# Spectra by pairs of k1, one step for k1 = 32, raw weights on another queue: a change to a fused S4D convolution and gated unit

## The chip, the cores and the metric

The kernel runs on one NeuronCore of a Trainium2 chip. TensorE (PE) multiplies matrices into PSUM, VectorE (DVE), ScalarE (ACT) and GpSimd (POOL) work elementwise, and SyncE (SP) issues DMAs. ACT and POOL issue DMAs as well, each from a queue of its own. Every engine takes its instructions in the program's order. The metric is device time in microseconds (us); the profile is one execution, as the hardware profiler recorded it.

## The reference

The input `u` has 2048 positions of 448 channels. It is normalized, and two branches are added to it.

```python
xn = _layernorm(x)
# S4D: a kernel of 2048 taps for each channel, from 256 complex modes
P = exp((A * dt[:, None])[:, :, None] * pos[None, None, :])
K = 2.0 * einsum("dn,dnl->dl", C, P).real
y = irfft(rfft(xn_t, 2 * L) * rfft(K, 2 * L))[..., :L]      # causal convolution
a = y + xn * D_skip
# gated unit: 448 -> 1792 -> 448
b = (sigmoid(xn @ w_gate) * (xn @ w_up)) @ w_down
out = x + a + b
```

All inputs and the output are float32.

## The kernel before

Two generators in Python emit the program. `conv()` emits the convolution, `glu()` the gated unit. The loop at the end of the kernel always advances the one whose done share of its total is smaller; each `yield` carries a weight (`WK`, `WS`, `WP`, `WX` and so on) that is added to what is done. So the weights and the two totals decide how the two branches lie beside each other on PE. A scheduler then orders the instructions of each engine from that emission; `issue_after` pins some of them behind a named instruction.

**The convolution.** The transform of 4096 points is split in 64 x 64. `x_pair` and `x_spec` make the first stage of the input's transform and store it as `x1_d`. `rest(q)` loads blocks 8 to 15 of the input early and takes their statistics with `x_stats`. `kgen` generates the taps in 56 chunks: POOL builds magnitudes (`me`, `mf`, line 467), ACT sines (`S`), DVE their products `Et` and `Ft` (lines 520 to 522), and PE multiplies these into `ko` (line 532). After every fourth chunk the taps get their skip term (line 545, `ks`) and go through the first stage of their transform (line 559) to `sk_d`.

`spectra` does the rest for each half `h` of the channels (224 each) and for the 33 values of k1. A step has four values of k1; k1 = 32 is a step by itself in each half, so there are 18 steps. In a step `loads` fetches the two first-stage spectra (`sx`, `skl`) and a table; `there` transforms both (line 808), copies the taps' part to SBUF (`kc`, line 815), multiplies on DVE (lines 823 to 825); `back` transforms the product back (line 838), copies it (`vt`, line 845) and stores it from ACT's queue to `v_d` (line 854). `back` of a step is emitted ahead of `there` of the next. `turned` loads `v_d` into another layout (line 860), and `last` does the final transform of a half (line 871) and adds it to the result.

The bank of PSUM that `there` fills holds one part (real or imaginary) of two values of k1 for each 64 partitions. Six operations follow, each on 448 columns: four products, a subtraction, an addition.

**The gated unit.** The positions are worked on in two halves of 1024 and the 1792 hidden columns in 14 tiles of 128, in groups of 3, 3, 3, 3 and 2. `gate` runs 22 matmuls for each tile and 512 positions (line 638; float32 is split in a high and a low part), then tanh, product and split on ACT and DVE. Line 738 projects down after each group. In the first half the split weights are stored (`wt_d`, `dt_d`) and in the second reloaded, except for the tiles in `RAW`: their raw weights are loaded again on SP's queue (lines 576 to 584) and split on POOL (lines 692 to 715). One buffer, `wraw`, serves raw gate, up and down weights of all these tiles in turn. `ORDER` gives the groups' order in each half. Near the end of the second half the gated unit yields `None` and is held until the convolution has emitted everything.

Of the kernel before, what the change touches and what calls it, by code (L numbers as in the profile page):

```python
# [30 lines left out]
WS = 4  # L31
HOLE = 6
WS = 4
# [12 lines left out]
RAW = set(GROUPS[0] + GROUPS[1])  # L46
ORDER = [GROUPS, GROUPS[2:] + GROUPS[:2]]
# [8 lines left out]
def _tables():  # L56
# [17 lines left out]
    for q in range(NK1):  # L74
# [52 lines left out]
def s4d_glu_kernel(ctx, tc, io):  # L127
# [442 lines left out]
    def w_load(f, raw=None):  # L570
# [3 lines left out]
        for i, nm in enumerate(("B_w_gate", "B_w_up")):  # L574
            w = io[nm]
            nc.sync.dma_start(raw[:, i, 0:3], w[0:384, fs].rearrange("(k p) f -> p k f", p=128))
            for h in range(2):
                nc.sync.dma_start(raw[64 * h : 64 * h + 64, i, 3], w[384:448, fs])
        return raw

    def rd_load(f, rd=None):
        if rd is None:
            rd = pg.tile([128, D], F32, name="rd", bufs=RB)
        nc.sync.dma_start(rd, io["B_w_down"][128 * f : 128 * f + 128])
# [72 lines left out]
    def glu():  # L657
        for half in range(2):
# [4 lines left out]
            for fs_ in ORDER[half]:  # L663
# [10 lines left out]
                for f, t in order:  # L674
                    if t == 0:
# [14 lines left out]
                        elif f in RAW:  # L690
                            raw, wl = w_load(f), w_low()
# [8 lines left out]
                    if t == 0:  # L700
# [62 lines left out]
    def spectra(pf):  # L763
# [9 lines left out]
        def loads(h, k):  # L773
            ds, gs = slice(H * h, H * h + H), slice(7 * h, 7 * h + 7)
            sx = pf.tile([128, 4, H], F32, name="sx", bufs=NLD)
            sk = pf.tile([128, 7, 4, 32], F32, name="skl", bufs=NLD)
            if k == 32:
                nc.sync.dma_start(sx[:64, 0], x1_d[32, :, ds])
                nc.sync.dma_start(sk[:, :, 0], sk_d[:, gs, 32])
                return t32, sk, sx  # L780
            nc.sync.dma_start(sx[0:64], x1_d[k : k + 4, :, ds].rearrange("k b d -> b k d"))
# [13 lines left out]
        def there(k, ks, tb, sk, sx):  # L795

            np_, nj = (128, 2) if len(ks) > 1 else (64, 1)
            sp = {}
            for src, tag in ((sk, "ko"), (sx, "tr")):
                for c in range(2):  # L800
                    ps = bank("sp")
                    with after():
                        for n, (k1, i, j) in enumerate(ks):
                            kk = 64 if k1 in (0, 32) else 128
                            to, rhs = ps[64 * i : 64 * i + 64, j], sx[:kk, n]
                            if tag == "ko":
                                to, rhs = to.rearrange("p (g d) -> p g d", d=32), sk[:kk, :, n]
                            mm = nc.tensor.matmul(  # L808
                                to, tb[:kk, n, 64 * c : 64 * c + 64], rhs, start=True, stop=True,
                                skip_group_check=True,  # L810
                            )
                    sp_mm[:] = [mm]
                    if tag == "ko":
                        kc = pf.tile([128, 2, H], F32, name="kc", bufs=3)
                        nc.scalar.copy(kc[:np_, :nj], ps[:np_, :nj])  # L815
                        ps = kc
                    sp[tag, c] = ps
            o = (slice(0, np_), slice(0, nj))
            ys_ = [pf.tile([128, 2, H], F32, name="yy", bufs=4) for _ in range(2)]
            pd = [pf.tile([128, 2, H], F32, name="pd", bufs=2) for _ in range(2)]  # L820
            for c, to in ((0, ys_), (1, pd)):
                for e in range(2):
                    v.tensor_tensor(to[(c + e) % 2][o], sp["ko", e][o], sp["tr", c][o], ALU.mult)  # L823
            v.tensor_tensor(ys_[0][o], ys_[0][o], pd[0][o], ALU.subtract)
            v.tensor_tensor(ys_[1][o], ys_[1][o], pd[1][o], ALU.add)
            return ys_

        def back(h, k, ks, ys_):
            vt = pf.tile([128, 2, 2, H], F32, name="vt", bufs=2)
            bt = t32[:, 1:3] if k == 32 else bk  # L830
            n = min(2, len(ks))
            pvs = [bank("pv") for _ in range(n)]
            for p in range(0, len(ks), 2):
                for e in range(2):
                    for k1, i, j in ks[p : p + 2]:
                        s = slice(64 * i, 64 * i + 64)
                        with after():
                            mm = nc.tensor.matmul(  # L838
                                pvs[i][:, j], bt[s, e], ys_[e][s, j], start=(e == 0), stop=(e == 1),
                                skip_group_check=True,  # L840
                            )
                    sp_mm[:] = [mm]
            for i in range(n):
                nj = 2 if n == 2 else 1
                nc.scalar.copy(vt[:, i, :nj], pvs[i][:, :nj])


            for k1, i, j in ks:
                r = 32 if k1 == 32 else 8 * (k1 % 4) + k1 // 4
                if k1 in (0, 32):  # L850
                    to, fr = v_d[h, r::64], vt[0:128:2, i, j]
                else:
                    to, fr = v_d[h, r::32], vt[:, i, j]
# [199 lines left out]
```

## Time and profile before

| quantity | value |
|---|---|
| median of 3 runs | 843.39 us (840.48 to 846.02) |
| the profiled execution | 842.75 us, span 841.0 us |
| PE busy | 746.3 us, 89% of the span |
| DVE busy | 570.4 us, 68% |
| ACT busy | 401.1 us, 48% |
| POOL busy | 385.9 us, 46% |
| granted PE clock, mean | 0.939 |
| DMA | 112.83 MB, 134 GB/s in the mean |

The span runs from the first to the last instruction; the profiled execution has 1.75 us around it. The start lasts until the chunks of `kgen` begin near 140 us, these run to 608 us, the steps of `spectra` from 616 to 817 us, and the end to 841 us. PE and PEld are matmuls and their weight loads; a float32 matmul leaves two records, so eight matmuls stand as x16. The granted clock is the share of full speed that PE was given.

### The profile page before, as it was taken

To read this page: it belongs to the slowest core of one execution; us is meant where nothing else is said; L and a number is where in the kernel's file an instruction comes from. 1 tells how busy PE (TensorE), PEld (TensorE's weight loads), DVE (VectorE), ACT (ScalarE), POOL (GpSimd) and SP (SyncE) were. 2 spreads that over 40 slices of the span, in tenths; PEclk is the share of its full clock that TensorE was granted. 3 is DMA by queue.
4 is the path that set the end of the run, shared out by engine and by line. 5 is a ranking of instruction groups with operands and counts; after the bars stand their busy time and mean duration, and the time that the engine had idled before them with its cause. 6 is when DMAs were issued, how large, how long until landed. Compare 5 with 4: busy or idle time off the path is not lost.

```text
span 841.0 us, 18294 instructions
## 1 busy us (share of the span) xinstructions
PE 746.3 (89%) x7416; PEld 575.0 (68%) x7416; DVE 570.4 (68%) x766; ACT 401.1 (48%) x615; POOL 385.9 (46%) x390
## 2 busy tenths in 40 slices
PE   1999969988998987999999999999979998899766
PEld 1767758767886865666788778887746776466544
DVE  5598887887688989587489777789513443443333
ACT  2647445646658476675565666646412222122110
POOL 1100256875986996646376867778210021100002
PEclk9998979989999998699999999999979999699888
DMA  9444563343144443357432221220398898567536
GB/s 215 116 122 122 143 193 120 117 148 107 39 144 140 129 129 100 78 167 201 156 109 67 103 85 56 70 69 27 98 262 216 216 222 201 134 165 184 145 90 167
DMA packets 94467, 112.83 MB, mean 134 GB/s; under 512 B 12320, under 2 KB 83104, under 8 KB 94000
## 3 DMA queue, kind: packets, MB, share of 16 engines
q1 hardware_dynamic: 80272, 91.46, 39.9%
q10 hardware_dynamic: 13328, 18.47, 6.8%
q0 software_dynamic: 784, 1.74, 0.7%
q8 instruction: 58, 0.95, 0.5%
q14 instruction: 25, 0.20, 0.1%
HBM read 69.07 MB, written 42.57 MB: 133 GB/s over the span
## 4 chain that ended last, share of the span: by engine, by line
PE 49%; DVE 15%; DMA 9%; issue 8%; ACT 7%; POOL 7%; ACTq 2%; SPq 1%; POOLq 0%; DVEq 0%
PE gu L638 19%; PE po L738 8%; PE tr L483 5%; PE ko L532 4%; PE sp L808 4%; PE pv L838 4%; POOL me L467 3%; PE kp L559 3%; DVE Et L521 2%; ACTq L854 2%; DVE Et L520 2%; DVE Ft L522 2%; DMA wraw<-in_B_w_up_dram 1%; DVE pm L408 1%; DMA acc_d<-acc 1%
## 5 line engine op out<-in xcount | busy, mean ns | idle before, releaser
L467 POOL TENSOR_TENSOR me<-me,pm 128x32 f32<-128x32 f32 (+3 forms) x168 | 170.0, 1014 | 95.9 <-DVE Et L521 81.0
L467 POOL TENSOR_TENSOR mf<-mf,pm 128x64 f32<-128x64 f32 (+3 forms) x112 | 127.8, 1143 | 5.6
L638 PE MATMUL gu<-xh,wh 128*128 128x512 f32 x336 | 103.5, 414 | 7.4 <-DVE hf L647 6.9
L520 DVE TENSOR_TENSOR Et<-me,S 128x1024 f32<-128x1024 f32 x56 | 88.5, 1580 | 31.4 <-ACT S L495 28.0
L638 PE MATMUL gu<-xh,wl 128*128 128x512 f32 x336 | 98.6, 400 | 0.0
L638 PE MATMUL gu<-xl,wh 128*128 128x512 f32 x336 | 96.4, 393 | 0.0
L522 DVE TENSOR_TENSOR Ft<-mf,S 128x1024 f32<-128x1024 f32 x56 | 86.0, 1536 | 9.9 <-PE ko L532 7.6
L823 DVE TENSOR_TENSOR yy<-kc,sp 128x448 f32<-128x448 f32 (+1 forms) x36 | 20.8, 590 | 106.0 <-ACT kc L815 88.5
L738 PE MATMUL po<-dh,hh 128*128 128x448 f32 x224 | 84.9, 379 | 3.7 <-DVE hf L647 1.9
L638 PEld LDWEIGHTS gu<-xh,wh 128*128 128x128 f32 x336 | 63.8, 197 | 29.3 <-DVE hf L647 7.4
L738 PE MATMUL po<-dl,hh 128*128 128x448 f32 x224 | 83.4, 373 | 0.0
L521 DVE TENSOR_TENSOR Et<-me,S 128x1024 f32<-128x1024 f32 x56 | 82.9, 1480 | 0.7 <-POOL mf L467 0.7
L738 PE MATMUL po<-dh,hl 128*128 128x448 f32 x224 | 82.8, 372 | 0.1
L492 ACT ACTIVATE S<-tr 128x1024 f32<-128x1024 f32 x56 | 57.5, 1027 | 50.3 <-PE tr L483 47.0
L483 PE MATMUL tr<-sel,ph 128*128 128x512 f32 x224 | 69.7, 433 | 9.0 <-ACT S L494 8.6
L638 PEld LDWEIGHTS gu<-xh,wl 128*128 128x128 f32 x336 | 65.1, 194 | 14.5
L638 PEld LDWEIGHTS gu<-xl,wh 128*128 128x128 f32 x336 | 63.7, 190 | 13.6
L532 PEld LDWEIGHTS ko<-Et,Ft 128*32 128x32 f32 x3584 | 56.2, 112 | 23.5 <-issue 15.8
L532 PE MATMUL ko<-Et,Ft 128*32 128x64 f32 x3584 | 68.2, 224 | 2.8 <-DVE Ft L522 2.8
L743 DVE SCALAR_TENSOR_TENSOR acc<-po,acc 128x448 f32<-128x448 f32 x80 | 48.2, 616 | 29.2 <-PE po L738 28.2
L495 ACT ACTIVATE S<-S,hpi 128x1024 f32<-128x1024 f32 x56 | 65.4, 1167 | 0.0
L652 ACT CAST hh<-hf 128x512 fp32r<-128x512 f32 x56 | 34.8, 622 | 63.0 <-DVE hf L647 61.0
(176 smaller groups left out, 1265.9 us busy)
## 6 DMA issues: line engine op xcount, KB each, us to landing
sk_d<-sk ACTq DMA_DIRECT2D x14, 528.0 KB
sx<-x_d SPq DMA_DIRECT2D x32, 224.0 KB
skl<-sk_d SPq DMA_DIRECT2D x16, 448.0 KB
vp<-v_d SPq DMA_DIRECT2D x16, 448.0 KB
v_d<-vt ACTq DMA_DIRECT2D x62, 112.0 KB
wt_d<-wh SPq DMA_DIRECT2D x8, 512.0 KB
wt_d<-wl SPq DMA_DIRECT2D x8, 512.0 KB
wh<-wt_d SPq DMA_DIRECT2D x8, 512.0 KB
```

The costliest lines, as they stand in the source:

```text
L467: nc.gpsimd.tensor_tensor(m[:, :, w : 2 * w], m[:, :, 0:w], par(base + i).unsqueeze(2).to_broadcast([128, 4 * DC, w]), ALU.mult,)
L483: nc.tensor.matmul(ps[:, h], ph[:, cn % 2, 128 * h : 128 * h + 128], sel[:, i], start=(i == 0), stop=(i == 1),)
L492: nc.scalar.activation(rows(cs), pv, AF.Abs)
L495: nc.scalar.activation(cs, cs, AF.Sin, scale=-TWO_PI, bias=hpi)
L520: v.tensor_tensor(Et[:, :, :, 32:64], two(me[:, :, 32:64]), S[:, 1::-1], ALU.mult)
L521: v.tensor_tensor(Et[:, :, :, 0:32], two(me[:, :, 0:32]), S[:, 1:3, :, ::-1], ALU.mult)
L522: v.tensor_tensor(Ft, two(mf), S[:, 3:5], ALU.mult)
L532: nc.tensor.matmul(ko[32 * j : 32 * j + 32, sl], Ft[:, cc, DC * h + 4 * q + j], Et[:, cc, DC * h + 4 * q + j], start=(k == 0), stop=(k == ...
L638: glu_mm[:] = [nc.tensor.matmul(ps, a_, b_, start=(n == 0), stop=(n == len(mm) - 1))]
L652: nc.scalar.copy(hh, hf)
L738: glu_mm[:] = [nc.tensor.matmul(po, a_[:, bs], w_, start=(n == 0), stop=(n == 3 * fc - 1))]
L743: v.scalar_tensor_tensor(acc[:, b], po, 0.5, acc[:, b], ALU.mult, ALU.add)
```

## The change

Six edits are made together.

1. In a step of `spectra` the values of k1 go by pairs: a bank holds both parts of one pair. The taps' copy `kc`, the products and the sums are made for each pair. Two products of 448 columns give both parts' terms (one reads the bank with its parts swapped), and a subtraction and an addition of 224 columns combine them: eight operations a step in place of six.
2. k1 = 0 uses 128 rows like the others; its table has zeros in the lower 64.
3. k1 = 32 is one step for both halves of the channels, the second of 17 steps.
4. Raw weights of the second half are loaded from POOL's queue. `RAW` loses its fourth tile, and the second half does group 1 before group 0.
5. `rest` is a generator: its load is issued a turn earlier, and its statistics follow in the next turn, behind the last gate's product.
6. `WS` goes from 4 to 4.5, and the convolution's total counts 11 preparation turns and 17 steps in place of 9 and 18.

```diff
-WS = 4
+WS = 4.5
...
-RAW = set(GROUPS[0] + GROUPS[1])
-ORDER = [GROUPS, GROUPS[2:] + GROUPS[:2]]
+RAW = set(GROUPS[0] + GROUPS[1][1:])
+ORDER = [GROUPS, GROUPS[2:] + GROUPS[1::-1]]
...
+    tab[0, 64:] = 0.0
...
-                            raw, wl = w_load(f), w_low()
+                            raw, wl = w_load(f, eng=nc.gpsimd), w_low()
...
-                            rd = rd_load(f, pg.tile([128, D], F32, name="rdw", tag="wraw", bufs=1))
+                            rd = rd_load(f, pg.tile([128, D], F32, name="rdw", tag="wraw", bufs=1), nc.gpsimd)
...
             if k == 32:
-                nc.sync.dma_start(sx[:64, 0], x1_d[32, :, ds])
-                nc.sync.dma_start(sk[:, :, 0], sk_d[:, gs, 32])
+                nc.sync.dma_start(sx[:64, 0:2].rearrange("b h d -> b (h d)"), x1_d[32])
+                for i in range(2):
+                    nc.sync.dma_start(sk[:64, :, i], sk_d[:64, 7 * i : 7 * i + 7, 32])
                 return t32, sk, sx
...
+        def there(k, tb, sk, sx):
+            kk, np_ = (64, 64) if k == 32 else (128, 128)
+            ys_ = []
+            for j in range(2):
+                ks = [(0, j, 0)] if k == 32 else [(2 * j + i, 2 * j + i, i) for i in range(2)]
+                pss = []
+                for src in (sk, sx):
+                    ps = bank("sp")
+                    with after():
+                        for c in range(2):
+                            for t, n, i in ks:
+                                to, rhs = ps[64 * i : 64 * i + 64, c], sx[:kk, n]
+                                if src is sk:
+                                    to, rhs = to.rearrange("p (g d) -> p g d", d=32), sk[:kk, :, n]
+                                mm = nc.tensor.matmul(
+                                    to, tb[:kk, t, 64 * c : 64 * c + 64], rhs, start=True, stop=True,
+                                    skip_group_check=True,
+                                )
+                    sp_mm[:] = [mm]
+                    pss.append(ps)
+                    if src is sk:
+                        kc = pf.tile([128, 2, H], F32, name="kc", bufs=3)
+                        nc.scalar.copy(kc[:np_], ps[:np_])
+                yy = pf.tile([128, 2, H], F32, name="yy", bufs=4)
+                pd = pf.tile([128, 2, H], F32, name="pd", bufs=2)
+                xt = pss[1]
+                v.tensor_tensor(yy[:np_], kc[:np_], xt[:np_], ALU.mult)
+                v.tensor_tensor(pd[:np_], kc[:np_], xt[:np_, ::-1], ALU.mult)
+                v.tensor_tensor(yy[:np_, 0], yy[:np_, 0], yy[:np_, 1], ALU.subtract)
+                v.tensor_tensor(yy[:np_, 1], pd[:np_, 0], pd[:np_, 1], ALU.add)
+                ys_.append(yy)
+            return ys_
...
-        steps = [(h, k) for h in range(2) for k in (32, *range(0, 32, 4))]
+        steps = [(h, k) for h in range(2) for k in range(0, 32, 4)]
+        steps[0:2] = [steps[1], (None, 32), steps[0]]
...
                     x_load(xt, 4 * q, 4, [nc.sync])
-                    for b in range(4):
-                        x_stats(sm, 4 * q + b, xt[:, b])
+                    yield
+                    with tc.issue_after(hfs[-1].ins):
+                        for b in range(4):
+                            x_stats(sm, 4 * q + b, xt[:, b])
+                    yield
...
-                    if n in (5, 7):
-                        rest((n - 1) // 2)
+                    if n in (4, 6):
+                        more = rest(n // 2)
+                    if n >= 4:
+                        next(more, None)
...
-    total = [sum(Y0) + 9 * WP + 8 * WX + 4 + NCK * WK + HOLE + 18 * WS, 2 * (4 + NFT * 14.8) - HELD]
+    total = [sum(Y0) + 11 * WP + 8 * WX + 4 + NCK * WK + HOLE + 17 * WS, 2 * (4 + NFT * 14.8) - HELD]
```

More of the change, by code (lines that the diff above doesn't have):

```diff
@@ L30 @@
 WK = 5
-WS = 4
+WS = 4.5
 HOLE = 6
-WS = 4
+WS = 4.5
 WP = 5
@@ L568, in kgen, with w_load @@
                 yield WK
-    def w_load(f, raw=None):
+    def w_load(f, raw=None, eng=nc.sync):
         fs = slice(128 * f, 128 * f + 128)
@@ new lines, in there, with back @@
+                v.tensor_tensor(yy[:np_, 0], yy[:np_, 0], yy[:np_, 1], ALU.subtract)
+                v.tensor_tensor(yy[:np_, 1], pd[:np_, 0], pd[:np_, 1], ALU.add)
+                ys_.append(yy)
+            return ys_
+        def back(h, k, ys_):
+            vt = pf.tile([128, 2, 2, H], F32, name="vt", bufs=2)
+            bt, n = (t32[:, 1:3], 1) if k == 32 else (bk, 2)
+            pvs = [bank("pv") for _ in range(n)]
+            with after():
+                for j in range(2):
+                    for e in range(2):
+                        for i in range(n):
+                            s = slice(64 * i, 64 * i + 64)
@@ L817, in there @@
[L817 to L842, printed above, removed]
-            for i in range(n):
[L844 to L853, printed above, removed]
-                nc.scalar.dma_start(to.rearrange("r w d -> w r d"), fr)
@@ new lines, in back @@
+            sp_mm[:] = [mm]
+            for i in range(n):
+                nc.scalar.copy(vt[:, i], pvs[i])
+            for j in range(2):
+                for i in range(n):
+                    k1 = k + 2 * j + i
+                    if k == 32:
+                        to, fr = v_d[j, 32::64], vt[0:128:2, 0, j]
+                    elif k1 == 0:
+                        to, fr = v_d[h, 0::64], vt[0:128:2, i, j]
+                    else:
+                        to, fr = v_d[h, 8 * (k1 % 4) + k1 // 4 :: 32], vt[:, i, j]
+                    nc.scalar.dma_start(to.rearrange("r w d -> w r d"), fr)
@@ L894, in spectra @@
         for n, (h, k) in enumerate(steps):
-            ks = [(32, 0, 0)] if k == 32 else [(k + 2 * j + i, i, j) for j in range(2) for i in range(2)]
             sp_mm[:] = glu_mm
@@ L899, in spectra @@
                 back(*prev)
-            cur = there(k, ks, *ld[n])
+            cur = there(k, *ld[n])
             if n + NLD < len(steps):
```

31 lines of the change are left out of this document (8 added, 23 removed).

## The prediction

> **What bounds the kernel now.** I read the page first, then the busy time in stretches of 20 us, then the chain of work that ended last, and the timeline of single steps.
>
> ```profile
> span 841.0 us, 18294 instructions
> PE 746.3 (89%) x7416; PEld 575.0 (68%) x7416; DVE 570.4 (68%) x766; ACT 401.1 (48%) x615; POOL 385.9 (46%) x390
> PEclk9998979989999998699999999999979999699888
> ```
> ```profile
> 480.00:500.00 20.00, 20.00 (x264) 15.99 (x253) 15.78 (x14) 13.32 (x19) 16.84 (x15) 1.00 0.25 91
> 800.00:820.00 20.00, 12.51 (x78) 10.28 (x79) 7.19 (x13) 3.61 (x8) 0.00 (x0) 0.83 0.32 85
> ```
>
> PE is the bound, but not everywhere. In the kernel-generation stage (columns: window, busy PE, PEld, DVE, ACT, POOL, clock, DMA share, GB/s) it has no free moment from 480 to 500. At 800 to 820 it is idle for 7.5 us of 20 and runs at 0.83 of its clock. So time is to be had late, in the spectra, and the chain there shows why:
>
> ```profile
> 616.55 3.21 PE sp L808 x8
> 626.30 0.95 PE pv L838 x4
> ...
> 665.48 1.80 PE pv L838 x16
> ...
> 674.94 1.78 PE pv L838 x16
> ...
> 687.00 3.18 PE sp L808 x32
> 690.18 5.21 PE gu L638 x22
> ...
> 717.79 1.52 PE pv L838 x4
> 719.32 10.48 PE sp L808 x32
> ...
> 733.47 1.71 PE pv L838 x16
> ...
> 743.58 1.76 PE pv L838 x16
> ...
> 757.44 1.76 PE pv L838 x16
> ...
> 773.77 1.76 PE pv L838 x16
> ...
> 794.61 1.80 PE pv L838 x16
> ...
> 803.54 3.38 PE pv L838 x16
> ...
> 814.03 3.28 PE pv L838 x16
> ```
>
> Each row of L838 is one step's transform back (start, length). Eighteen steps take from 616.55 to 814.03: 197.5 us. A step beside 22 gate matmuls (G22) lasts 10.1 us (733.47 to 743.58); one beside 18 down-projections (P18) 9.5 (665.48 to 674.94); one beside nothing 8.9 (794.61 to 803.54). So nearly all of a step is a chain of its own, which GLU work merely fills:
>
> ```profile
> 695.32 1.78 PE L838 MATMUL pv<-yy,bk 64*128 64x224 f32 x16
> 697.14 0.97 ACT L845 COPY vt<-pv 128x448 f32<-128x448 f32 x2 [1.11 <-PE pv L838]
> 697.70 3.25 ACTq L854 DMA_DIRECT2D v_d<-vt  x4
> 700.99 0.97 ACT L815 COPY kc<-sp 128x448 f32<-128x448 f32 x2 [2.89 <-DMA v_d<-vt]
> 704.83 0.61 DVE L824 TENSOR_TENSOR yy<-yy,pd 128x448 f32<-128x448 f32 x1
> 705.59 1.78 PE L838 MATMUL pv<-yy,bk 64*128 64x224 f32 x16 [2.58 <-DVE yy L824]
> ```
>
> Transform back, two evacuations, four stores that hold ACT for 3.25 us, the copies kc, six DVE operations, transform back: 10.3 us, here with eleven gate matmuls (G11). The number of steps, not their size, is what costs.
>
> **The change part by part.** The program's order is counted for the changed kernel too; it has the same 4,814 PE matmuls.
>
> *One step fewer, other cover.* k1 = 32 is done once, so there are 17 steps. The changed order on PE gives the GLU work beside each step after the first: G22, G11, G22, G22, P18, P18, P18, P18+G11, G11, G22, G22 and G11 with the final transforms of half 0, G22, G22, G11, P18. Before, the last two steps had nothing. By the rows above: the first two 9.5 each (the single step is short), G22 10.1, P18 9.5, G11 10.3. P18+G11 is limited by PE: 1.78 + 3.18 + 11 x 5.21/22 + 18 x 5.21/22 x 448/512 = 11.3. The two steps with the final transforms are 13.9 and 16.3 (743.58 to 757.44 to 773.77), kept. The sixteen sum to 169.6. The first stretch was 9.75 (616.55 to 626.30); now a full step opens on a cold clock (8 opening rows took 3.21, as long as 32 warm ones), so I add 2 (0 to 4): 11.8. The tail from the last transform back to the end holds the same work (8 transforms, 54 down-projections, 64 final transforms): 27.0, unchanged.
>
> *Products by pairs.* Four multiplications of 448 columns stay; two combinations of 448 become four of 224. A 64x224 one took 0.37 below, against 0.61: 4 x 0.37 - 2 x 0.61 = +0.26 us a step. It counts on the eight or so steps that PE does not limit: +2.1 (0 to 4.4). The first pair's products can start before the second pair's transforms, but ACT still does stores ahead of kc, so I count no gain. k1 = 0 on 128 rows streams the same columns: nothing.
>
> *The port.* Those combinations read two SBUF operands, and POOL's raw splits now lie almost all in this stage:
>
> ```profile
> 714.76 2.35 POOL L693 TENSOR_TENSOR wl<-wraw,wh 128x1024 fp32r<-128x1024 f32 x1
> 714.85 2.50 DVE L825 TENSOR_TENSOR yy<-yy,pd 64x224 f32<-64x224 f32 x1
> 717.27 0.37 DVE L824 TENSOR_TENSOR yy<-yy,pd 64x224 f32<-64x224 f32 x1
> ```
>
> The same combination took 2.50 under the split and 0.37 after it. Two more splits than before fall among the steps: +2 x 2.1 = 4.2 (0 to 4.2 and, with what follows, rival C). The Trainium skill (SBUF — State Buffer, "Who interferes with whom") says that a VectorE instruction with two SBUF inputs is blocked for the whole of a GpSimd instruction that reads SBUF; the rows agree, and by the rule every meeting costs up to the whole split, which would add another 4 us here.
>
> *Raw weights by POOL's queue.* 42 DMAs leave SP; 35, seven a tile, come to POOL, in front of its own work.
>
> ```profile
> L219 POOL DMA_DIRECT2D out_dram<-acc x5 | 2.7, 551 | 72.6 <-DVE acc L743 72.2 <-DVE acc L879 0.5
> out_dram<-acc POOLq DMA_DIRECT2D x5, 112.0 KB, 4.7
> 713.64 1.04 POOL L692 CAST wh<-wraw 128x1024 fp32r<-128x1024 f32 x1 [12.58 <-DMA v_d<-vt]
> SPq L584 <- POOL wl L693: 11.7, 2, 8.2
> ```
>
> On SP a down-projection load waited up to 8.2 us for POOL, with the spectra's loads queued behind it; conversely a split waited 12.58 us for weights. On POOL the same waits follow POOL's own work. An issue costs 0.55 us of POOL and lands in 4.7, so one raw tile takes 7 x 0.55 + 4.7 + 1.04 + 2.35 + 4.7 + about 1.5 (the smaller split, by its columns) = 18 us, and its gates take two to four steps, 20 us or more: hidden. The first of these loads stands in POOL's queue in mid-generation, ahead of the next magnitudes, and waits there for the spectrum stores out of the same buffer; POOL's free time covers it (0; rival D if not). The gain on SP is in the steps already. One tile becomes stored and reloaded: four stores and four loads at a DMA share of 0.25, nothing.
>
> *Pace.* WS and the totals move 56 gate matmuls from the generation into the spectra, where the chain covers them. Time per four chunks, by the addition that ends each:
>
> ```profile
> 319.18 0.16 DVE L545 TENSOR_TENSOR ks<-ko,dm 128x8 f32<-128x8 f32 x1
> 349.08 0.16 DVE L545 TENSOR_TENSOR ks<-ko,dm 128x8 f32<-128x8 f32 x1
> 387.45 0.16 DVE L545 TENSOR_TENSOR ks<-ko,dm 128x8 f32<-128x8 f32 x1
> 424.39 0.16 DVE L545 TENSOR_TENSOR ks<-ko,dm 128x8 f32<-128x8 f32 x1
> ...
> 484.68 0.16 DVE L545 TENSOR_TENSOR ks<-ko,dm 128x8 f32<-128x8 f32 x1
> 515.69 0.16 DVE L545 TENSOR_TENSOR ks<-ko,dm 128x8 f32<-128x8 f32 x1
> ```
>
> A group with 84 GLU matmuls takes 31.0 us. The sixth has 22, and 28 for the normalized input: 29.9. The seventh has 46 and 34: 38.4. The eighth has 110: 36.9. Now the sixth and seventh have 22 and 16 each: 29 each (between 20, PE alone, 31.0 - 46 x 0.237, and 29.9; nearest the row of 29.9, for DVE has the same work): -0.9 and -9.4. The eighth has 29 GLU fewer (x 0.237 = -6.9) and 30 input matmuls more (0 to 0.237 each; half: +3.6): -3.3. The ninth has 17 more: +4.0. The rest balance. Sum -9.6; bounds 0 and -13.3 (56 x 0.237).
>
> *Statistics of the later input.* Their load is issued one turn ahead, and they are queued behind the last gate's product.
>
> ```profile
> DVE st L227 <- DMA xn<-in_A_u_dram: 2.5, 1, 2.5
> ```
>
> DVE waited 2.5 us there, with the gate's product behind it: -2 (0 to -2.5).
>
> **Sum.** Spectra: 11.8 + 169.6 + 2.1 + 4.2 + 2 (the opening step's first load is four times as large; 0 to 4) = 189.7 against 197.5: -7.8. Generation -9.6, statistics -2: -19.4. Against the span: 841.0 - 19.4 = 821.6. The profiled execution took 842.75, 1.75 around its span: 823.4. The median shown is 0.64 above that execution: **824 us**. By its own bounds this case goes from 808 to 836.
>
> **The rivals.** *B, moved but not saved:* the light groups of the generation are set by DVE (it makes Et and Ft whatever PE does), so taking GLU work away shortens nothing and the statistics merely wait elsewhere. For it: the sixth group still took 29.9 with a quarter of the GLU work. Against: all groups of 84 and more lie on a full PE. 824 + 9.6 + 2 = 836.
>
> *C, the port with the clock:* POOL's four later splits each catch the combinations, PE idles about 3 us, and the clock drops, as at 717.79, after which 16 transforms took 10.48 instead of 3.18. Price 4 x (2.1 + 7.3) - 4.2 = 33: 857. Against: other such splits passed without it, and G22 now covers those steps.
>
> *D, late weights (slower):* POOL's queue is in order, and one buffer serves gate and down weights alike. With DMA full, landings of 15 us make a tile take 39 us; from one tile's gates to the next's are three steps, 30 us, so PE, in order too, waits 9 us at three tiles, with one cold stretch: 824 + 27 + 7 = 858. It decides from a landing of 11 us. For it: 12.58 above. Against: that wait was behind SP's other loads, and POOLq landed in 4.7. The Trainium skill (DMA: Bandwidth & Descriptors, "Issuing engines are not separate DMA queues") says that issuing from another engine saves only the issue time, since all share the 16 DMA engines; by it a full DMA stays full and D would keep the 12.58, at 843. No row shows POOL's loads under that load.
>
> *E, a warm clock:* cover everywhere keeps the clock up and the extras of the spectra vanish: 824 - 8.3 - 6 = 810 or less.
>
> **How the numbers follow.** Forecast 0.58, B 0.17, C 0.08, D 0.12, E 0.05. A measurement of this kernel tells about 1% from no change, 8.4 us. Faster: the forecast, E and part of B, 0.70. Same: the rest of B and mild C or D, 0.15. Slower: 0.15. The range runs from 805, past E, to 846, past B; it leaves out the full C and D.
>
> **What would show it.** Right: 17 transforms back, about 10 us apart, with no sp row of 10 us in mid-stage; the first sp row near 605; the sixth and seventh groups near 29 us; SP with no wait for POOL's split. Wrong: PE idle over 3 us before gates whose wl is late (D); combinations of 2 us or more (C); the first sp row still near 616 (B); last transform back later than 800.

## The result, and the profile after

| kernel | median us (lowest to highest) | ratio to the kernel before, 95% interval |
|---|---|---|
| before | 843.89 (840.48 to 846.02) | 1 |
| changed | 816.45 (814.80 to 819.14) | 0.9682 (0.964 to 0.9724) |

The change makes the kernel 27 us faster, 3.2%. The forecast was 824 with a range of 805 to 846. A second measurement of the changed kernel, on another chip, gave 817.05 and a ratio of 0.9756 (0.9711 to 0.9801); the kernel before had 838.67 there. So its own time hardly moves between these two chips, that of the kernel before more. The profiled execution of the changed kernel took 819.14 us, the longest of its four; that of the kernel before took 842.75, near its median. The stretches below are those of the two profiled executions.

The page of the changed kernel, its span, busy times and granted clock:

```profile
span 817.4 us, 18309 instructions
PE 721.9 (88%) x7416; PEld 563.8 (69%) x7416; DVE 572.2 (70%) x794; ACT 400.6 (49%) x612; POOL 392.7 (48%) x421
PEclk9999989999999998887999999999989999999998
```

PE does the same work in 24.4 us less busy time (746.3 before) and is idle as long as before: 95.5 us against 94.7. By an estimate from the mean clocks, 0.960 against 0.939, 16 us of this are the clock. The 7, the 6 and most of the 8s of the last eleven slices have gone from the row; two 8s stay. What is left is a dip (8887) from 306 to 388 us, in the generation, where the kernel before had one too (86).

The same two windows as before, the second moved to where the last steps now lie (window, PE, PEld, DVE, ACT, POOL, clock, DMA share, GB/s):

```profile
480.00:500.00 20.00, 20.00 (x227) 15.99 (x227) 14.24 (x15) 14.06 (x20) 15.94 (x14) 1.00 0.27 92
780.00:800.00 20.00, 19.07 (x121) 15.13 (x120) 9.97 (x22) 3.52 (x7) 1.09 (x2) 1.00 0.47 120
```

The last steps have work beside them and the full clock; before, PE was busy for 12.5 us of 20 there, at 0.83. Over the whole of the spectra (first line before, second changed) PE's idle time falls from 25.9 to 10.2 us and the clock rises from 0.91 to 0.98:

```profile
616.55:814.03 197.48, 171.61 (x1170) 122.00 (x1171) 79.59 (x142) 41.94 (x84) 13.09 (x12) 0.91 0.75 188
612.58:791.08 178.50, 168.29 (x1227) 123.90 (x1227) 89.08 (x173) 43.94 (x86) 34.91 (x40) 0.98 0.81 206
```

The chain of work that ended last, from the end of the generation on:

```profile
605.07 7.38 DMA skl<-sk_d
612.58 4.84 PE sp L815 x32
622.64 1.71 PE pv L843 x16
...
653.44 1.72 PE pv L843 x16
655.16 3.18 PE sp L815 x32
663.55 1.76 PE pv L843 x16
673.82 1.53 PE pv L843 x12
...
704.51 1.76 PE pv L843 x16
715.04 2.61 PE pv L843 x12
717.66 3.49 PE sp L815 x32
726.36 1.76 PE pv L843 x16
...
740.29 1.76 PE pv L843 x16
...
751.74 1.71 PE pv L843 x16
...
782.67 1.41 PE pv L843 x12
...
791.08 2.00 PE pv L843 x16
```

There is no row of 10 us for 32 transforms any more; the longest in mid-stage is 3.49. Seventeen steps take from 612.58 to 791.08, 178.5 us, against 197.5. The generation, by the addition that ends four chunks:

```profile
185.28 0.16 DVE L547 TENSOR_TENSOR ks<-ko,dm 128x8 f32<-128x8 f32 x1
...
342.98 0.16 DVE L547 TENSOR_TENSOR ks<-ko,dm 128x8 f32<-128x8 f32 x1
374.60 0.17 DVE L547 TENSOR_TENSOR ks<-ko,dm 128x8 f32<-128x8 f32 x1
421.28 0.17 DVE L547 TENSOR_TENSOR ks<-ko,dm 128x8 f32<-128x8 f32 x1
...
598.74 0.17 DVE L547 TENSOR_TENSOR ks<-ko,dm 128x8 f32<-128x8 f32 x1 [2.03 <-ACT ks L546]
```

The first addition comes at 185.28 (189.00 before) and the last 413.5 us later (414.7 before). The seventh group got shorter, 31.6 us for 38.4, and the eighth longer by more, 46.7 for 36.9. From the first addition to the last, PE is busy for 11.3 us less than before and idle for 10.1 us more (first line before, second changed):

```profile
189.00:603.70 414.70, 393.77 (x5069) 311.09 (x5068) 329.84 (x342) 259.70 (x374) 291.25 (x280) 0.97 0.33 104
185.28:598.74 413.46, 382.46 (x5031) 305.24 (x5031) 323.05 (x341) 256.21 (x368) 285.50 (x286) 0.96 0.35 109
```

| stretch | before | changed | moved | forecast |
|---|---|---|---|---|
| start to first addition | 189.0 | 185.3 | -3.7 | -2 |
| first to last addition | 414.7 | 413.5 | -1.3 | -9.6 |
| last addition to first transform | 12.8 | 13.8 | +1.0 | in the next row (+2) |
| spectra | 197.5 | 178.5 | -19.0 | -7.8 |
| tail | 27.0 | 26.3 | -0.7 | 0 |
| span | 841.0 | 817.4 | -23.6 | -19.4 |

The sum was nearly right, its parts were not. Two of these rows are too small to read. Five profiles have the changed kernel's order on PE up to the spectra: this one and four among the runs below (its repeat, products by parts, raw weights on SP's queue, stores behind the copies). In them the first addition comes between 182.4 and 188.9 us, and the additions take 411.6 to 415.5. The start's -3.7 and the generation's -1.3 lie inside such differences.

The experiments ask which edits carry the gain.

### The profile page after: what moved, and what is told of

Its sections match the earlier page's. It is cut to its first block, busy times and chain, and to the rows that moved or that the text cites. A ratio compares the mean times of both kernels' runs of the same rounds, so it can differ in the third digit from the quotient of the medians.

```text
span 817.4 us, 18309 instructions
## 1 busy us (share of the span) xinstructions
PE 721.9 (88%) x7416; PEld 563.8 (69%) x7416; DVE 572.2 (70%) x794; ACT 400.6 (49%) x612; POOL 392.7 (48%) x421
## 4 chain that ended last, share of the span: by engine, by line
PE 53%; DVE 15%; DMA 8%; ACT 7%; issue 7%; POOL 5%; SPq 2%; ACTq 2%; DVEq 0%; POOLq 0%
PE gu L640 19%; PE po L740 11%; PE ko L534 5%; PE tr L485 5%; PE pv L843 3%; PE kp L561 3%; PE sp L815 3%; POOL me L469 3%; DVE Et L523 2%; DMA v_d<-vt 2%; ACTq L861 1%; DVE pm L410 1%; DVE Et L522 1%; DVE pd L828 1%; POOL mf L469 1%
## 5 line engine op out<-in xcount | busy, mean ns | idle before, releaser
L469 POOL TENSOR_TENSOR mf<-mf,pm 128x64 f32<-128x64 f32 (+3 forms) x112 | 119.0, 1064 | 6.1
L640 PE MATMUL gu<-xh,wh 128*128 128x512 f32 x336 | 99.8, 402 | 5.6 <-DVE hf L649 5.2
L522 DVE TENSOR_TENSOR Et<-me,S 128x1024 f32<-128x1024 f32 x56 | 85.8, 1532 | 23.8 <-ACT S L497 22.1
L640 PE MATMUL gu<-xh,wl 128*128 128x512 f32 x336 | 96.2, 393 | 0.0
L524 DVE TENSOR_TENSOR Ft<-mf,S 128x1024 f32<-128x1024 f32 x56 | 82.6, 1476 | 14.7 <-PE ko L534 10.0
L523 DVE TENSOR_TENSOR Et<-me,S 128x1024 f32<-128x1024 f32 x56 | 87.4, 1561 | 0.3 <-ACT S L497 0.3
L534 PEld LDWEIGHTS ko<-Et,Ft 128*32 128x32 f32 x3584 | 58.1, 115 | 32.4 <-issue 17.3
L534 PE MATMUL ko<-Et,Ft 128*32 128x64 f32 x3584 | 70.3, 228 | 10.7 <-DVE Ft L524 10.7
L640 PEld LDWEIGHTS gu<-xh,wh 128*128 128x128 f32 x336 | 61.9, 190 | 24.7 <-DVE hf L649 5.7
L640 PEld LDWEIGHTS gu<-xh,wl 128*128 128x128 f32 x336 | 63.4, 189 | 13.6
L485 PE MATMUL tr<-sel,ph 128*128 128x512 f32 x224 | 67.5, 422 | 5.0 <-ACT S L496 3.3
```

Of the source, the lines that this page charges most:

```text
L469: nc.gpsimd.tensor_tensor(m[:, :, w : 2 * w], m[:, :, 0:w], par(base + i).unsqueeze(2).to_broadcast([128, 4 * DC, w]), ALU.mult,)
L485: nc.tensor.matmul(ps[:, h], ph[:, cn % 2, 128 * h : 128 * h + 128], sel[:, i], start=(i == 0), stop=(i == 1),)
L522: v.tensor_tensor(Et[:, :, :, 32:64], two(me[:, :, 32:64]), S[:, 1::-1], ALU.mult)
L523: v.tensor_tensor(Et[:, :, :, 0:32], two(me[:, :, 0:32]), S[:, 1:3, :, ::-1], ALU.mult)
L524: v.tensor_tensor(Ft, two(mf), S[:, 3:5], ALU.mult)
L534: nc.tensor.matmul(ko[32 * j : 32 * j + 32, sl], Ft[:, cc, DC * h + 4 * q + j], Et[:, cc, DC * h + 4 * q + j], start=(k == 0), stop=(k == ...
```

## The experiments: edits undone one at a time

Runs of one group share a chip and the runs of the kernel before. In the first group that kernel has a median of 839.22.

**Two single steps.** k1 = 32 has a step in each half of the channels again, so there are 18.

```diff
-                nc.sync.dma_start(sx[:64, 0:2].rearrange("b h d -> b (h d)"), x1_d[32])
+                nc.sync.dma_start(sx[:64, 0], x1_d[32, :, H * h : H * h + H])
...
-        steps[0:2] = [steps[1], (None, 32), steps[0]]
+        steps[0:2] = [steps[1], (0, 32), steps[0]]
+        steps[9:9] = [(1, 32)]
```

> The changed kernel with k1 = 32 again a step of its own in each half (18 steps, weights of the totals to match). The changed kernel took 816.5 us. Theory 'chain': a step costs its chain of some 9 to 10 us whatever its size, so one more step gives about 824 to 826. Rival 'disturbance': what the old single steps cost was only the cold clock and the blocked combination in mid-stage; covered by gate matmuls a single step costs its PE work alone (under 3 us): 817 to 819.

Measured: 816.31 (814.62 to 817.94), ratio 0.9751 (0.9688 to 0.9813). No loss, so it looked as if the number of steps did not count. The run with the old statistics, further below, spoils this reading.

**Products by parts.** `there` as before: a bank holds one part, six operations a step.

```diff
-            for j in range(2):
...
+            for src, tag in ((sk, "ko"), (sx, "tr")):
+                for c in range(2):
+                    ps = bank("sp")
...
+            v.tensor_tensor(ys_[0][:np_], ys_[0][:np_], pd[0][:np_], ALU.subtract)
+            v.tensor_tensor(ys_[1][:np_], ys_[1][:np_], pd[1][:np_], ALU.add)
```

> The changed kernel with products by parts again (a bank holds one part of two values of k1, six DVE operations of 448 columns), still 17 steps. Theory 'chain': ACT makes both copies kc only after four stores, so the pairs gain nothing and their two extra operations cost little: 815 to 818. Rival 'pairs': the first pair's early products shorten every step that PE does not limit by half a us or more: 820 or above.

Measured: 817.28 (813.72 to 820.14), ratio 0.9774 (0.9692 to 0.9856). Outside the transforms themselves PE's order is the same as in the changed kernel, so this is a clean undo. The pairs neither gain nor cost anything that stands out of the 6 us between its runs; the spectra of its profile take 177.8 us against 178.5.

**The old pace.**

```diff
-WS = 4.5
+WS = 4
...
-    total = [sum(Y0) + 11 * WP + ...
+    total = [sum(Y0) + 9 * WP + ...
```

> The changed kernel with the old pace (WS = 4, total with 9 preparation turns): 66 fewer gate and down matmuls lie in the spectra, and its last two steps have none. Theory 'chain': the generation hardly got shorter when work was taken from it (1.3 us between its first and last skip addition), so giving it back costs it 1 to 3 us, and the uncovered steps run at their chain: 816 to 820. Rival 'pace': the moved work is worth its PE time, 66 x 0.237 = 16 us, and cold stretches return: 828 or above.

Measured: 830.51 (827.76 to 841.57), ratio 0.9926 (0.9882 to 0.997). Of the edits undone so far only this one gives the gain back, most of it. In its trace the first addition comes 8 us later than in the changed kernel, and the generation takes as long:

```profile
193.34 0.16 DVE L547 TENSOR_TENSOR ks<-ko,dm 128x8 f32<-128x8 f32 x1
```

By the order on PE, 29 more gate matmuls lie ahead of that point than in the changed kernel; at the 0.237 us of the prediction they are 6.9 of the 8.1 us. So an earlier or later first addition mostly says where matmuls were put, and not that anything was saved.

Its spectra take 177.9 us, as long as in the changed kernel, with 66 matmuls of the gated unit fewer beside them (255 for 321, by the trace). So the new pace lays 66 matmuls, 15.6 us at 0.237, beside spectra that don't get longer for it; between the two kernels' times, on two chips, are 14 us. And the 8.7 us that this run keeps against the kernel before are what the other five edits bring without the pace: their spectra are 19.6 us shorter than before, while 18 more matmuls of the gated unit lie ahead of the first addition (537 for 519, 4.3 us). Which of the five shortens the spectra isn't separated by it.

**Raw weights on SP's queue again.**

```diff
-                            raw, wl = w_load(f, eng=nc.gpsimd), w_low()
+                            raw, wl = w_load(f), w_low()
...
-                            rd = rd_load(f, pg.tile([128, D], F32, name="rdw", tag="wraw", bufs=1), nc.gpsimd)
+                            rd = rd_load(f, pg.tile([128, D], F32, name="rdw", tag="wraw", bufs=1))
```

> The changed kernel with the raw weights on SP's queue again. Theory 'queue': waits for POOL on SP hold the spectra's loads, and some steps come late: 819 to 823. Rival 'issue only': the loads run three steps ahead and lose nothing: 815 to 818.

Measured: 817.59 (814.76 to 820.07), ratio 0.9765 (0.9698 to 0.9832). No difference that shows, again with PE's order unchanged. This undoes only the queue: no run goes back on `RAW` and `ORDER` in the changed kernel.

## The experiments: edits put into the kernel before

The kernel before had a median of 839.98 on this chip.

**Only the raw weights on POOL's queue**, by the same four lines, the other way round.

> The kernel before, with one thing changed: the raw weights of the second half are loaded from POOL's queue instead of SP's. PE's order is that of before. Theory 'disturbance': most of the 19 us that the spectra lost is the stretch around the single step of the second half in the kernel before, where raw loads on SP's queue, POOL's split, a blocked combination and a cold clock came together (27.8 us for two steps, 14.8 in the run with two single steps). Then this alone removes that stretch: spectra 183 to 187 us, time 828 to 834. Rival 'pace': the stretch comes from how the gated unit lies beside the steps, which is unchanged here; then 838 to 846, spectra 195 to 199.

Measured: 835.78 (833.34 to 842.47), ratio 0.9967 (0.9933 to 1.0001), between the two theories. The stretch around the single step went from 27.8 to 20.2 us, and the spectra of its profile, which is of its fastest run, from 197.5 to 189.2. PE's order is that of the kernel before, and the row that took 10.48 us took 5.68. So in this profile the meeting in the middle is gone, and with it 8 us of the spectra, yet it isn't the bulk; the interval of the whole time still touches 1.

**Only the new pace.**

```diff
-WS = 4
+WS = 4.5
...
-    total = [sum(Y0) + 9 * WP + ...
+    total = [sum(Y0) + 11 * WP + ...
```

> The kernel before, with only the pace changed (WS 4.5, eleven preparation turns and eighteen steps in the total). Theory 'disturbance': the first skip addition comes 4 to 8 us sooner (the run with the old pace came 8 us later than the changed kernel), and the uncovered last steps, 10 us each on a cold clock, take 9 each; the meeting of raw loads and split stays, so spectra 190 to 196 and the time 828 to 836. Rival 'pace': pace does it all: first skip addition at 183 to 186, spectra 177 to 182, time 815 to 823. If pace does little outside the changed kernel: 838 or more.

Measured: 818.67 (812.50 to 823.09), ratio 0.9749 (0.9684 to 0.9815). Two numbers give nearly the whole gain of the change (a repeat, on the chip of the last group, gave 0.9764). Its chain:

```profile
604.44 3.21 PE sp L808 x8
613.98 0.95 PE pv L838 x4
...
707.62 0.99 PE pv L838 x4
708.61 5.68 PE sp L808 x32
...
791.20 1.78 PE pv L838 x16
```

The spectra begin 12 us sooner than before (604.44 for 616.55) and take 186.8 us for 197.5, though 66 more matmuls of the gated unit lie beside them. The row at 708.61 answers to the one that took 10.48 in the kernel before: 20 matmuls of the gated unit stand ahead of it, no large split meets the combinations before it, and it takes 5.68.

That is not a milder stall. These are the transforms of the step that has k1 = 0, and in the kernel before its other half takes 5.68 for them as well. The windows of both, with the clock in the third column from the end, and then the first rows of such a step and of an ordinary one (a row names the shape of its first record):

```profile
627.25:632.93 5.68, 5.68 (x33) 2.64 (x33) 1.84 (x3) 1.93 (x4) 0.00 (x0) 1.00 1.06 262
719.32:729.80 10.48, 10.48 (x33) 4.16 (x33) 2.80 (x3) 1.93 (x4) 1.69 (x2) 0.50 0.56 136
```
```profile
627.18 2.91 PE L808 MATMUL sp<-skl,tb 64*64 64x224 f32 x16
735.11 1.73 PE L808 MATMUL sp<-skl,tb 128*64 128x224 f32 x16
```

A quarter of the records of such a step are matmuls of 64 rows, mixed with those of 128. With 128 rows throughout, as in the changed kernel, the transforms of this step take 3.2 us in both halves, as long as those of any other. In the second half of the run with two single steps, and in both halves of the one with products by parts, they take 3.2 as well, so neither the pairs nor the single step makes the difference. Edit 2 thus saves 2.5 us of PE in each half. How much of it reaches the whole time isn't known, as no run undoes edit 2 alone. Of the 7.3 us between 10.48 and 3.18, then, 2.5 are the shape and 4.8 the clock, 0.50 instead of 1.00.

**Both.**

> The kernel before with both: raw weights from POOL's queue and the new pace. The other four edits (pairs of k1, 128 rows for k1 = 0, one step for k1 = 32, later statistics, order of the groups and one tile less) are left out. Each of them, undone in the changed kernel so far, brought nothing back; if these two carry the change, 814 to 821 and spectra 176 to 182. If the transforms' edits carry part that hides behind each other, 824 to 832.

Measured: 822.18 (819.93 to 822.68), ratio 0.9791 (0.9744 to 0.9838), between the two ranges again. With the new pace POOL's queue adds no gain that shows.

**Stores behind the copies.** The changed kernel, with ACT's four stores of a step queued behind both copies `kc` of the next.

```diff
-                    nc.scalar.dma_start(to.rearrange("r w d -> w r d"), fr)
+                    with tc.issue_after(kcs[0].ins):
+                        nc.scalar.dma_start(to.rearrange("r w d -> w r d"), fr)
...
-                back(*prev)
+                bk_ = back(*prev)
+                next(bk_)
...
+            if prev is not None:
+                next(bk_, None)
```

> The changed kernel, with the four stores of a step (3.25 us of ACT's queue) behind both copies kc of the next step instead of ahead of them. Theory 'chain' (the prediction's: a step is a chain of its own through ACT): the copies come 3 us sooner, and the eight or so steps that PE does not fill get 2 to 3 us shorter each: 792 to 802. Rival 'PE fills the steps': beside 22 gate matmuls a step is 10.2 us of PE alone, so only the steps beside 11 or 18 gain, about 1 us each: 808 to 813. Rival 'the copies wait for the transforms anyway' (sp is emitted behind the gate matmuls): 814 to 819.

Measured: 808.76 (808.45 to 815.01), ratio 0.9654 (0.9598 to 0.971). PE's order is that of the changed kernel in every group and step. The changed kernel did not run on this chip, but it took 816.45 and 817.05 on the two where it did, so the gain is about 8 us. ACT's timeline of the same step, first in the changed kernel, then here:

```profile
645.51 0.96 ACT L849 COPY vt<-pv 128x448 f32<-128x448 f32 x2
646.07 2.52 ACTq L861 DMA_DIRECT2D v_d<-vt  x4
648.63 0.97 ACT L823 COPY kc<-sp 128x448 f32<-128x448 f32 x2 [2.16 <-DMA v_d<-vt]
```
```profile
646.73 0.97 ACT L850 COPY vt<-pv 128x448 f32<-128x448 f32 x2 [0.37 <-PE pv L844]
647.66 0.53 ACT L824 COPY kc<-sp 128x448 f32<-128x448 f32 x1
649.23 0.53 ACT L824 COPY kc<-sp 128x448 f32<-128x448 f32 x1 [1.04 <-PE sp L816]
649.30 1.83 ACTq L864 DMA_DIRECT2D v_d<-vt  x3
```

The first copy follows at once instead of 2.2 us later, and the stores go out while DVE multiplies. The spectra take 169.6 us for 178.5, in the longest of the runs (815.0). The chain of the prediction is thus real, but it gave 9 us and not 15 or more; the rival 'PE fills the steps' had the size. A step beside 22 gate matmuls still lasts 10.1 us, as PE is busy all through it.

## The experiments: what is left beside the pace

All on one chip, the kernel before at 838.67.

**The changed kernel and the pace alone, side by side.**

> The changed kernel itself, beside the next three on one chip. Measured before: ratio 0.968 to the kernel before. Theory 'the edits add up' (pace 0.975 alone, the other five 0.993): it stays 0.5 to 1% below the pace alone, at 811 to 815 where the kernel before has 840. Rival 'pace is all': within 0.3% of the pace alone, 816 to 820.

> The kernel before with the new pace alone, again, to be held against the changed kernel on the same chip. Both theories: 816 to 821 where the kernel before has 840 (ratio 0.975 measured).

Measured: 817.05 (815.78 to 818.61) and 817.78 (815.85 to 820.94). They are the same within the spread. Taken by itself this says that the other five edits do nothing. The run with the old pace, and the next one, show that this is wrong. In the profile of the pace alone repeated, of its slowest run, the spectra take 191.0 us for the 186.8 above: in it a combination of the step behind the single one did meet a split and took 2.78 us, and this step's transforms took 7.28 at a clock of 0.77. PE's order is the same in both, so the meeting in the middle can come or stay away from one execution to the next.

**The old statistics.** The changed kernel with edit 5 undone.

```diff
-                    yield
-                    with tc.issue_after(hfs[-1].ins):
-                        for b in range(4):
-                            x_stats(sm, 4 * q + b, xt[:, b])
-                    yield
+                    for b in range(4):
+                        x_stats(sm, 4 * q + b, xt[:, b])
...
-                    if n in (4, 6):
-                        more = rest(n // 2)
-                    if n >= 4:
-                        next(more, None)
+                    if n in (5, 7):
+                        rest((n - 1) // 2)
```

> The changed kernel with the statistics of the later input as before (load and statistics in one turn, after turns 5 and 7), the new totals kept. The prediction's term: 2 us at the start come back, first skip addition at 187 instead of 185, time 2 above the changed kernel. Rival 'the start is the pace's alone': no difference, first skip addition 183 to 186.

Measured: 805.79 (804.38 to 809.04), ratio 0.9626 (0.9584 to 0.9668). Neither theory expected it: with this one edit undone the kernel is 11 us faster than the changed kernel, a gain of 3.7% instead of 2.4% on this chip. Between the two profiles of this chip the first addition comes 5.8 us later without the edit (190.2 for 184.4), the additions take 13.3 us less (400.7 for 414.0) and the spectra 4.0 less (172.8 for 176.8). The first two belong together: 35 more gate matmuls lie ahead of the first addition, 8 us at 0.237, and are then missing behind it. So up to the last addition 7.5 us are saved, and the rest in the spectra.

What PE waited for between 342 and 376 us, first in the changed kernel (the profile shown above, whose groups are those of the repeat), then here (engine, line, what it waited for: us, times, longest):

```profile
PE kp L561 <- DVE ks L547: 9.3, 2, 5.4
PE ko L534 <- DVE Ft L524: 7.4, 1, 7.4
```
```profile
PE tr L485 <- ACT S L496: 1.6, 1, 1.6
PE ko L534 <- DVE Ft L524: 0.7, 1, 0.7
```

And both in the window from 340 to 380, in the same sequence:

```profile
340.00:380.00 40.00, 25.54 (x410) 18.76 (x412) 31.67 (x39) 22.68 (x38) 27.25 (x32) 0.76 0.24 69
```
```profile
340.00:380.00 40.00, 37.68 (x417) 25.34 (x410) 31.95 (x38) 26.39 (x44) 30.66 (x33) 0.74 0.36 100
```

In the changed kernel PE stands idle for 14 us of these 40, where the first half of the gated unit has ended and little of the second is there to fill in: 16.7 us of waits against 2.3. DVE, ACT and POOL are about as busy in both. But the 14 us are not all lost work. PE has 410 records in the one window and 417 in the other, at nearly the same clock, and they count as 25.5 us busy in the one and 37.7 in the other. Without the edit the lead near 375 us is smaller than that: 12 matmuls of the gated unit and 16 records of the second half's input more are done. The eighth group then holds 104 and 24 of them instead of 120 and 40, has a clock of 1.00 instead of 0.94, and takes 38.4 us instead of 46.7, on a PE that is full in both. By estimates, 16 matmuls at 0.237 are 3.8 of these 8.3 us, and the clock is 2.8.

The two orders on PE differ well ahead of that. With the edit 508 matmuls of the gated unit come before the end of the first four chunks on PE, without it 543; the fifth group has 72 of them and none that load the second half's input, against 51 and 8. All this follows from an edit to two loads and sixteen small DVE operations; how the scheduler comes from the one to the other was not followed. The spectra have the same order of PE; the rows there show fewer waits of PE for the combinations (4.8 us for 7.4 in the repeat), and no run separates them further. The 51 and 8 alone don't make a kernel fast: the runs with the old pace and with the pace alone have them too.

This also corrects the first experiment. The kernel with two single steps drew an order like that of this last one (51 and 8 in the fifth group; 5 us of waits between 342 and 376), not that of the changed kernel. Its 816.3 is to be held against 805.8 rather than 816.5, and its spectra's 178.9 us against 172.8: a step more then costs some 6 to 10 us. The two ran on different chips and no run shows this with the order held fixed, so it stays open between nothing and 10.

**Stores behind the copies, and more pace.** WS 5 in place of 4.5.

```diff
-WS = 4.5
+WS = 5
```

> The changed kernel with the stores behind the copies (808.8 measured) and WS 5 instead of 4.5: 22 more matmuls of the gated unit move from the generation into the spectra (397 instead of 375). Theory 'cover is what counts': with the shorter chain nearly every step beside 22 gate matmuls is full of PE work already (10.1 us a step), so the spectra grow by the moved work, 22 x 0.237 = 5, and the generation, which has idle PE near 370, gives back less: 809 to 815. Rival 'more pace, more gain': 800 to 807.

Measured: 803.43 (801.63 to 805.60), ratio 0.9594 (0.9553 to 0.9635): the fastest of all. Its order, too, has the favourable fifth group (51 and 8), and its spectra begin at 602.25 for 612.58, while they last 173.8 us, 4 more than with WS 4.5. So the spectra grew by about the moved work, as 'cover is what counts' had it, and yet the total fell by the other theory's size. The change of order may have done that; the two causes are not separated here, and the run it is held against was on another chip.

## Why the prediction was right, and where it was not

**Right by the sum, and by luck in it.** 816.45 lies 7.6 below the forecast and in its own range of 808 to 836. Two large terms were wrong in opposite directions, by 11 and 8 us, and nothing in the working made them cancel. Four terms:

- *The spectra, -7.8, measured -19.0.* The sixteen periods were forecast at 169.6 and took 168.4. The extras put on top did not show in that sum. The second step with final transforms took 11.45 (740.29 to 751.74) where 16.33 had been kept from before, though it now has 11 gate matmuls beside it and not 22. The opening stretch took 10.1 instead of 11.8. The first load, four times as large, does cost about what was forecast (7.38 us at 605.07 for 4.67 before), but it lies ahead of the first transform, where the table has +1.0. One term was put at nothing with a reason that the rows refute: k1 = 0 on 128 rows was to change nothing as it streams the same columns, and it takes 2.5 us of PE less in each half. The reason given for the gain, the number of steps, isn't shown. Two ways shorten the spectra, and they overlap: the other five edits without the pace bring 19.6 us (the old pace, 177.9), and the pace alone, which keeps 18 steps, brings 10.7 and carries 66 matmuls more.
- *The generation, -9.6, measured -1.3.* This is the step that failed. The term took every one of 56 moved matmuls as one less between the additions. By the trace the spectra have 55 more, but 16 of them come from the stretch between the last addition and the first transform and 3 from ahead of the first; between the additions 36 are fewer, 8.5 us at 0.237. PE's busy time there did fall, by 11.3 us, and its idle time rose by 10.1; its waits for the additions, from the first to the last, went from 6.0 to 16.9 us. Rival B had said this: another engine than PE sets the light groups. The sixth group came out as forecast (28.5 for 29), the seventh at 31.6 for 29, the eighth at 46.7 for 33.6. The eighth was to be 29 matmuls of the gated unit lighter by the order on PE; by the times of the additions it holds 10 more (120 for 110) and 40 records of input where it had none. The pace alone has 7.2 us of waits near 342 to 376 instead of 16.7 and saves 6.3 between the additions, two thirds of the term.
- *The statistics, -2, the wrong sign.* Costed from one wait of 2.5 us; the kernel with the edit takes 11 us longer than without. The 3.7 us at its start lie inside what five profiles of this order differ by. The prediction counted the order on PE, but only with all edits together, so it had no price for this edit through the order.
- *POOL's queue, nothing:* right, as far as the time of the changed kernel with and without it tells. The first raw load did stand in POOL's queue as described, and waited 7.0 us for the spectrum stores.

**The rivals.** C and D did not come. The port did block: two of the four large splits met combinations. One of these splits, then the combinations of both meetings, from the timeline of the changed kernel:

```profile
641.75 2.36 POOL L695 TENSOR_TENSOR wl<-wraw,wh 128x1024 fp32r<-128x1024 f32 x1
```
```profile
641.94 2.42 DVE L830 TENSOR_TENSOR yy<-pd 128x224 f32<-128x224 f32 x1
...
712.10 1.99 DVE L829 TENSOR_TENSOR yy<-yy 128x224 f32<-128x224 f32 x2
```

One combination took 2.42 under a split of 2.36, and two took 1.99, against 0.37 for one that is free: 2.05 and 1.25 more. That agrees with the rule of the Trainium skill (SBUF — State Buffer, "Who interferes with whom"). Three others took 0.91 to 1.34 beside POOL's casts and smaller splits, 2.4 more together. The kernel before had one meeting of 2.1, so the port cost DVE 3.6 more where the term had 4.2, and not all of it lies in the chain. The cold clock that C feared came in a small way, behind the second meeting: 0.83 from 712 to 722 us, and the rows at 715.04 and 717.66 took 2.61 and 3.49, 1.4 us more together than their like at a full clock, not 4.8. For D, POOL's loads landed in 3.5 to 4.9 us in the median, where it took 11 to decide for D. The splits waited 10.5 us for gate weights in two waits, 7.0 at most, where D had taken 12.58, and PE has no wait for a late `wl` among its longest. The rule that another issuing engine saves only the issue time (DMA: Bandwidth & Descriptors, "Issuing engines are not separate DMA queues", in the Trainium skill) held: 817.6 with SP's queue against 816.5 to 817.1. E, at 810, was a little nearer to the time than the forecast, and nearer in the spectra: less the extras and the 6 us that E takes off (the prediction has no row for the 6), the forecast's 189.7 would be 175.4, and 178.5 were measured, at a clock of 0.98 for 0.91.

**What would show it.** The seventeen transforms back, the missing 10 us row, the last one before 800 and SP without waits for POOL's split came as written. The first transform did not come near 605 but at 612.58, nearer to the 616 that the prediction had named as the sign of rival B.

## What to carry to other kernels

Where two branches are interleaved by weights, try the weights alone first: here two numbers gave what six edits together gave, because idle PE in a late stage took in work from an earlier one. An edit that changes the emission also changes the order everywhere else, so an undo is clean only if the order on the bounding engine is the same; compare that order before reading the time. And look for idle stretches of the bound engine at the seams between stages: here, matmuls taken out of a stretch that other engines set left idle time in their place.

## What the runs showed of the hardware

PE's busy time fell by 24.4 us with the same number of matmuls and the same idle time in the whole. Ends of matmuls are modelled, so this is what the profile counts. 11.0 us of it are in the spectra's first transforms, by their line (68.1 before, 57.1 changed). Of these 5 are the two steps with k1 = 0: 32 records took 5.68 us at full clock with matmuls of 64 and of 128 rows mixed, and 3.18 with 128 rows throughout.

In the seam of the generation the granted clock was 0.76 and 0.74 over 40 us in two kernels, with PE idle for 14 us of them in the one and for 2 in the other: what a wait there did to the clock can't be read from its length alone. Nor can the work be read from the busy time: 410 and 417 records counted as 25.5 and 37.7 us.
